# Block products that run on in two PSUM banks, running sums copied out by ScalarE, and low parts made in one piece

## The chip, the cores and the metric

The kernel runs on one core of a Trainium2 chip. The metric is device time in microseconds of one execution, the median of several runs. Lower is better.

## The reference, cut to what matters

Two branches over 2048 tokens of 576 features are mixed by a gate. One is a 2D Fourier filter. The other is a gated feed-forward layer with 4608 hidden features:

```python
x = A_x
g = _sigmoid((x * gate_w).sum(-1, keepdims=True))
a = irfft2(rfft2(x) * (A_w_r + 1j * A_w_i))
h = _gelu(B_x @ B_w_gate) * (B_x @ B_w_up)      # 2048 x 4608
b = h @ B_w_down                                # 2048 x 576
return g * a + (1 - g) * b
```

All inputs are fp32. The kernel splits an operand into a high part of 12 mantissa bits and a low part, the rest, and adds the products high x high, high x low and low x high.

## The kernel before, in words

Tokens stand in two halves of 1024, each as two groups (tb) of 512; hidden features in 36 tiles of 128. The first 900 us or so do the first token half plainly (all feature tiles), a few tiles of the second half, and the whole Fourier branch beside it on VectorE and ScalarE.

The rest of the second half is done in blocks, and only this stage is touched. A call of `products(i)`, for i = 5 to 17, takes two feature tiles and two token groups as a 2 x 2 block matrix product and does it with seven products in place of eight (a scheme of Winograd's kind): sums of the token side (a11, a12, a22, s1 to s4) were made once before, sums of the weight side are made block by block, and the four results c11, c12, c21, c22 are sums of products. Each product is done twice, for gate and for up (s = 0, 1), by `seven`: seven matmuls of 128x128 weights on 512 tokens into one PSUM bank. Six of them are high and low parts of two full feature tiles; the seventh takes the 64 features left over, high parts on partitions 0 to 63 and low parts on 64 to 127 (the tail). The weights stand in four slots of 1280 columns; `prep_b(i, m)` fills a slot two products ahead: `total` makes the weight sum on VectorE, `high` copies 768 columns to the rounded type on ScalarE, `low` makes the low parts on VectorE.

The banks are two of pool `pgu` and two of pool `pone`, taken in turn: product n uses the pair that product n - 2 used. VectorE adds each product to the running sums in SBUF (`add`, L1004). When a result is complete, `finish` queues gelu on the gate half (ScalarE), the multiplication by the up half (VectorE, L987), a rounded copy (ScalarE) and its low part (VectorE, L991). Behind a product come `downs`: a down is 12 matmuls of the hidden tiles of the block before on w_down into a pair of banks of pool `pdn` (L787), then a scaled copy out by ScalarE in `put` (L812) and an accumulating DMA from GpSimd's queue into the DRAM tile `yd` (L800). The last eight downs stand in `finale`: there the sums so far are loaded back from `yd` (`load_last`, SyncE's queue), VectorE adds to them in SBUF (L841), and SyncE's queue stores the result.

The order is written out by hand. Every engine executes its instructions in the order in which the program names them. `gap()`, called behind each half of a product and each down, counts up, and `seq(key, (n, step), ...)` names each step at the n-th gap from now (0 and 1 are both the next one); `due(key)` names what is left of a sequence at once.

Of the kernel before, what the change touches and what calls it, by code (L numbers as in the profile page):

```python
# [15 lines left out]
P = 128  # L16
# [15 lines left out]
FIRST = 5  # L32
# [125 lines left out]
def _build(nc, tc, a):  # L158
    with ExitStack() as ctx:
# [10 lines left out]
        def f(x):  # L170
            return x.bitcast(F32)
# [40 lines left out]
        def copy(o, i):  # L212
            act.activation(o, i, AF.Copy)  # L213
# [479 lines left out]
        def seq(key, *steps):  # L693

            q = todo[key] = [fn for _, fn in steps]
            for n, _ in steps:
                at(n, lambda: q and q.pop(0)())
# [264 lines left out]
        def seven(ps, i, m, x, s):  # L962

            due(("b", i, m))
            w, (xh, xl, xt) = slots[(7 * i + m) % 4], ops[x]
            hi, lo = w[:, 0:512], w[:, 768:1280]
            for t in range(2):
                c = slice(256 * t + P * s, 256 * t + P * (s + 1))
                pe.matmul(ps, hi[:, c], xh[:, t], start=t == 0, stop=False)  # L969
                pe.matmul(ps, lo[:, c], xh[:, t], start=False, stop=False)  # L970
                pe.matmul(ps, hi[:, c], xl[:, t], start=False, stop=False)  # L971
            pe.matmul(ps, w[:, 512 + P * s:512 + P * (s + 1)], xt, start=False, stop=True)  # L972
            tick(7 * 0.2265)
            gap()

        def products(i, spare, pend):

            j = NT + 2 * i
            u, c, u3 = gl, [xraw[:, q] for q in range(2)], [xraw[:, q] for q in range(2, 4)]
            made = {}  # L980

            def finish(name, x):
                h, (g, v) = spare.pop(0), x
                made[name] = h

                def mult():
                    vec.tensor_tensor(v, g, v, ALU.mult)  # L987
                    credit[0] -= 0.69

                def low():  # L990
                    vec.tensor_tensor(h[:, 1], v, f(h[:, 0]), ALU.subtract)  # L991
# [5 lines left out]
                if i == NT // 2 - 1 and name in ("c21", "c12"):  # L997
                    gelu()
                    seq((name, i), (1, mult), (1, lambda: copy(h[:, 0], v)), (2, low))
                else:  # L1000
                    seq((name, i), (1, gelu), (2, mult), (3, lambda: copy(h[:, 0], v)), (5, low))

            def add(o, x, v):
                vec.tensor_tensor(o, x, v, ALU.add)  # L1004
                credit[0] -= 0.69

            downs = (2, 2, 1, 1, 1, 1, 0) if i > FIRST else (1, 0, 1, 0, 1, 1, 0)
            for n, (name, nd) in enumerate(zip(("a11", "a12", "s2", "s3", "s1", "a22", "s4"), downs)):
                m = n + 2
                prep_b(i + m // 7, m % 7)  # L1010
                if n == 2:
                    for q in (0, 1, 3, 2):
                        load_b(i + 1, q)
                if n in (2, 3):
                    w = (j + n - 2) % 4
                    copy(dn[w][:, 0], wdr[n - 2])
                    lower(("dn", j + n - 2), dn[w], wdr[n - 2], 0.76)
                if n == 4:
                    due(("dn", j))
                    due(("dn", j + 1))  # L1020
                    load_d(i + 1)
                ps = [ps_one() if n % 2 else ps_gu() for _ in range(2)]
                for s in range(2):
                    seven(ps[s], i, n, name, s)
                    due({1: ("c12", i - 1), 3: ("c21", i - 1), 4: ("c11", i), 6: ("c22", i)}.get(n))
                    if n == 0:
                        copy(u[s], ps[s])
                    for o, x in (((), ((c, u),), ((u, u),), ((u3, u),), ((c, u3), (u, u)), ((u3, u3),), ((c, u),))[n]):
                        add(o[s], x[s], ps[s])
                k = {1: ("c11", c), 4: ("c22", c), 5: ("c21", u3), 6: ("c12", c)}.get(n)  # L1030
                if k:
                    finish(*k)
                for _ in range(nd):
                    if pend:
                        d, t = pend.pop(0)
                        down(d, t)
                        if t == 3 and len(d) > 4:
                            spare.extend(d[4])
                if i == NT // 2 - 1 and n == 5:
                    load_last(1)  # L1040
            for tb, names in ((1, ("c21", "c22")), (0, ("c11", "c12"))):
                hh = [made[q] for q in names]
                d = (1, i, tb, tuple((j + q, hh[q], (names[q], i)) for q in range(2)), hh)
                pend.extend((d, t) for t in range(4))

        def finale(pend):
            load_last(0)
            for d, t in pend[:4]:
                v = pair()
                for part in range(2):  # L1050
                    down_last(d, t, v, part)
                gap()
            d = pend[4][0]
            ps = [pair(), pair(), [ps_one()[:, 0:HD] for _ in range(2)], [ps_gu()[:, 0:HD] for _ in range(2)]]
            for part in range(2):
                for t in range(4):
                    down_last(d, t, ps[t], part)
# [197 lines left out]
```

## Time and profile before

| | |
|---|---|
| median of 3 runs | 1385.85 us (1384.22 to 1387.59) |
| span of the profiled execution | 1382.7 us; the page gives it no time of its own beside the span |
| TensorE busy | 1370.8 us, 99% |
| VectorE busy | 1119.5 us, 81% |
| ScalarE busy | 700.8 us, 51% |
| GpSimd busy | 265.4 us, 19% |

The span runs from the first to the last instruction; the rest of a run's time lies around it. PE is TensorE's matmuls, PEld its weight loads, DVE is VectorE, ACT ScalarE, POOL GpSimd, SP SyncE. Matmuls are pipelined: the duration of one is longer than the distance to the next.

### The profile page before, as it was taken

The numbers are of one execution on the slowest core, as the hardware profiler recorded it, in microseconds if no ns is written. First come the engines' busy times: TensorE is split into PE (matmuls) and PEld (weight loads), VectorE is DVE, ScalarE is ACT, GpSimd is POOL, SyncE is SP. The second block draws the span as 40 slices with busy tenths as digits, with TensorE's granted clock in tenths as the row PEclk, the third lists the DMA queues.
The fourth block names the chain that finished last, engine by engine and source line by source line (L and its number), as shares of the span: only waits on it lengthen the run. The fifth ranks groups of instructions, "written<-read, shape, count | busy, mean of one in ns | idle before, by whom it ended". The sixth has DMA issues, their size and how long they took to land.

```text
span 1382.7 us, 20005 instructions
## 1 busy us (share of the span) xinstructions
PE 1370.8 (99%) x7504; PEld 1211.0 (88%) x7504; DVE 1119.5 (81%) x1635; ACT 700.8 (51%) x1072; POOL 265.4 (19%) x326
## 2 busy tenths in 40 slices
PE   8999999999999999999999999999999999999998
PEld 7888888888888888888888888888888888888887
DVE  5999899989878877799988988557777777777776
ACT  5553443444566675543456345855555555555552
POOL 0022111122232221111113012321111121111110
PEclk9999999999999999999999999999999999999999
DMA  7366666657899997656678467966677777777776
GB/s 269 143 124 113 158 119 123 115 96 175 204 248 269 256 257 176 105 105 117 144 140 185 111 143 125 214 123 128 129 131 130 131 129 131 130 128 129 130 154 172
DMA packets 97330, 211.17 MB, mean 153 GB/s; under 512 B 11857, under 2 KB 22097, under 8 KB 96849
## 3 DMA queue, kind: packets, MB, share of 16 engines
q0 software_dynamic: 45248, 92.56, 44.4%
q1 hardware_dynamic: 51984, 117.34, 27.7%
q8 instruction: 59, 0.97, 0.3%
q14 instruction: 39, 0.31, 0.1%
HBM read 110.69 MB, written 92.01 MB: 147 GB/s over the span
## 4 chain that ended last, share of the span: by engine, by line
PE 85%; issue 6%; DVE 4%; ACT 1%; POOL 1%; DMA 1%; SPq 0%; DVEq 0%; POOLq 0%
PE pdn L787 29%; PE pgu L726 10%; PE pgu L728 10%; PE pgu L727 10%; PE pgu L969 3%; PE pgu L971 3%; PE pgu L970 3%; PE pone L969 3%; PE pone L971 3%; PE pone L970 3%; PE pgu L732 2%; PE pgu L733 2%; PE pgu L972 2%; PE pf L274 2%; PE pone L972 1%
## 5 line engine op out<-in xcount | busy, mean ns | idle before, releaser
L800 POOL DMA_DIRECT2D yd<-stg x264 | 229.1, 869 | 1043.4 <-ACT stg L812 922.0
L812 ACT ACTIVATE stg<-pdn,omg 128x576 f32<-128x576 f32 x272 | 201.7, 742 | 397.8 <-PE pdn L787 302.4
L787 PEld LDWEIGHTS pdn<-dn,hb 128*128 128x128 f32 x2808 | 388.6, 188 | 11.8 <-DVE raws L841 0.5
L787 PE MATMUL pdn<-dn,hb 128*128 128x288 f32 x2808 | 396.8, 295 | 0.2 <-DVE raws L841 0.2
L726 PE MATMUL pgu<-xhi,gu 128*128 128x512 f32 x728 | 285.5, 392 | 4.7 <-DVE gl L768 3.4
L728 PE MATMUL pgu<-xlo,gu 128*128 128x512 f32 x728 | 284.7, 391 | 0.0
L727 PE MATMUL pgu<-xhi,gu 128*128 128x512 f32 x728 | 284.3, 391 | 0.0
L726 PEld LDWEIGHTS pgu<-xhi,gu 128*128 128x128 f32 x728 | 137.1, 188 | 31.3 <-DVE gl L768 5.0
L728 PEld LDWEIGHTS pgu<-xlo,gu 128*128 128x128 f32 x728 | 137.1, 188 | 29.9
L727 PEld LDWEIGHTS pgu<-xhi,gu 128*128 128x128 f32 x728 | 136.9, 188 | 24.6
L213 ACT ACTIVATE hb<-gl 128x512 fp32r<-128x512 f32 x92 | 57.8, 628 | 111.0 <-DVE gl L768 110.6
L768 DVE TENSOR_TENSOR gl<-gl,pgu 128x512 f32<-128x512 f32 x92 | 62.9, 684 | 46.7 <-PE pgu L733 45.8
L764 ACT ACTIVATE gl<-pgu 128x512 f32<-128x512 f32 x91 | 54.3, 597 | 75.5 <-PE pgu L733 74.9
L213 ACT ACTIVATE gu<-raws 128x1280 fp32r<-128x1280 f32 (+3 forms) x86 | 88.6, 1031 | 5.9 <-DMA raws<-wgu 5.5
L787 PEld LDWEIGHTS pdn<-dn,gu 128*128 128x128 f32 x624 | 85.6, 188 | 1.9
L787 PE MATMUL pdn<-dn,gu 128*128 128x288 f32 x624 | 86.8, 295 | 0.0
L773 DVE TENSOR_TENSOR hb<-gl,hb 128x512 fp32r<-128x512 f32 x92 | 63.1, 686 | 16.5 <-ACT hb L213 16.5
L732 PE MATMUL pgu<-xtl,gu 128*128 128x512 f32 x182 | 70.9, 389 | 0.0
L733 PE MATMUL pgu<-xtl,gu 128*128 128x512 f32 x182 | 70.8, 389 | 0.0
L706 DVE TENSOR_TENSOR gu<-raws,gu 128x1280 fp32r<-128x1280 f32 x44 | 65.4, 1486 | 5.3 <-ACT gu L213 5.1
L987 DVE TENSOR_TENSOR xraw<-xraw 128x512 f32<-128x512 f32 x52 | 36.0, 693 | 28.8 <-ACT xraw L995 28.3
L1004 DVE TENSOR_TENSOR gl<-gl,pgu 128x512 f32<-128x512 f32 x52 | 35.6, 684 | 25.7 <-PE pgu L972 25.7
(213 smaller groups left out, 2214.6 us busy)
## 6 DMA issues: line engine op xcount, KB each, us to landing
yd<-stg POOLq DMA_DIRECT2D x264, 288.0 KB, 5.1
raws<-wgu SPq DMA_DIRECT2D x44, 640.0 KB, 4.9
raws<-wd SPq DMA_DIRECT2D x72, 288.0 KB, 2.9
colm<-col POOLq DMA_DIRECT2D x32, 256.0 KB, 6.2
raws<-ws SPq DMA_DIRECT2D x21, 384.0 KB, 6.0
quads<-ws SPq DMA_DIRECT2D x20, 384.0 KB, 4.2
tmp<-wf SPq DMA_DIRECT2D x16, 290.0 KB, 5.7
cns<-til SPq DMA_DIRECT2D x64, 72.5 KB, 5.4
```

Of the source, the lines that this page charges most:

```text
L213: act.activation(o, i, AF.Copy)
L726: pe.matmul(ps, w[:, 0, k, c], xhi[tb][:, k], start=k == 0, stop=False)
L727: pe.matmul(ps, w[:, 1, k, c], xhi[tb][:, k], start=False, stop=False)
L728: pe.matmul(ps, w[:, 0, k, c], xlo[tb][:, k], start=False, stop=False)
L732: pe.matmul(ps, w[:, 0, 4, c], xtl[tb], start=False, stop=False)
L733: pe.matmul(ps, w[:, 1, 4, c], xtl[tb], start=False, stop=True)
L787: pe.matmul(ps[half], h[:, l, c], d[:, q, half * HD:(half + 1) * HD], start=part == 0 and n == 0, stop=part == 1 and n == 2)
L800: pl.dma_start(yd[u], o, accum_op=ALU.add)
L812: put(u, lambda o: act.activation(o.rearrange("p (c k) -> p c k", c=2), v[:, :, 0:HD], AF.Copy, scale=omg[:, u:u + 1]), i == 0)
L969: pe.matmul(ps, hi[:, c], xh[:, t], start=t == 0, stop=False)
L970: pe.matmul(ps, lo[:, c], xh[:, t], start=False, stop=False)
L971: pe.matmul(ps, hi[:, c], xl[:, t], start=False, stop=False)
```

## The change

Four things change in the block stage. The order of the seven products and of the weight sums is another, and products run on: a11, s2, s3 and a22 add up in one pair of banks (b = 0), a12 in the other, which s1 and then s4 take over; from block to block the two pairs change places. Only the first product of a sum starts the bank anew. What was added in SBUF is now a sum in PSUM; where a running sum is wanted and the bank goes on, ScalarE copies it out (after products 0, 2 and 3), and VectorE adds only after products 1, 4 and 5. After the last product ScalarE takes the gelu straight from the bank, and VectorE multiplies by the other bank.

The slot's layout is low 0, high 0, tail, high 1, low 1 of 256 columns each, with the input tensor laid out to match. `high` copies 768 columns in the middle, `low` is one subtraction of 768 columns into pieces 0, 2 and 4, and a new step `tail`, one gap later, copies the high tail rows again on partitions 0 to 63 by ScalarE.

The downs stand behind other products, `finish` is called behind them, the weight loads for the next block one product later, and the two token groups of the finale change places, with the SBUF places that they are loaded to.

```diff
         def rest(i):
-            if i < 4:
-                return stg[i].rearrange("p c k -> p (c k)")
-            q = (2304, 2880, 1536, 0)[i - 4]
+            if i >= 4:
+                return stg[i - 4].rearrange("p c k -> p (c k)")
+            q = (2304, 2880, 0, 576)[i]
             return raws[:, q:q + D]
...
-            x = (r11, r21, tsum, r12, r11, r21, r22)[m]
+            x = (r11, r21, tsum, r11, r12, r22, r21)[m]
 
             def total():
-                for o, p, q in ((), (), ((r11, r12, r11), (tsum, r22, r11)), ((r12, r22, r12),), (),
-                                ((r21, r21, tsum),), ())[m]:
+                for o, p, q in ((), (), ((r11, r12, r11), (tsum, r22, r11)), (), ((r12, r22, r12),), (),
+                                ((r21, r21, tsum),))[m]:
                     vec.tensor_tensor(o, p, q, ALU.subtract)
                     credit[0] -= 0.95
 
             def high():
-                copy(w[:, 0:768], x)
+                copy(w[:, 256:1024], x)
 
             def low():
-                vec.tensor_tensor(w[:, 768:1280], x[:, 0:512], f(w[:, 0:512]), ALU.subtract)
-                vec.tensor_tensor(w[64:128, 512:768], x[64:128, 512:768], f(w[64:128, 512:768]), ALU.subtract)
-                credit[0] -= 1.15
-
-            seq(("b", i, m), (lead, total), (lead + 2, high), (lead + 4, low))
-
-        def seven(ps, i, m, x, s):
+                o = w.rearrange("p (c k) -> p c k", c=5)[:, 0:5:2]
+                vec.tensor_tensor(o, x.rearrange("p (c k) -> p c k", c=3),
+                                  f(w[:, 256:1024]).rearrange("p (c k) -> p c k", c=3), ALU.subtract)
+                credit[0] -= 0.95
+
+            def tail():
+                copy(w[0:64, 512:768], x[0:64, 256:512])
+
+            seq(("b", i, m), (lead, total), (lead + 2, high), (lead + 4, low), (lead + 5, tail))
+
+        def seven(ps, i, m, x, s, start, stop):
 
             due(("b", i, m))
             w, (xh, xl, xt) = slots[(7 * i + m) % 4], ops[x]
...
+            l0, h0, tl, h1, l1 = (w[:, 256 * q + P * s:256 * q + P * (s + 1)] for q in range(5))
+            for t, (hi, lo) in enumerate(((h0, l0), (h1, l1))):
+                pe.matmul(ps, hi, xh[:, t], start=start and t == 0, stop=False, skip_group_check=True)
+                pe.matmul(ps, lo, xh[:, t], start=False, stop=False, skip_group_check=True)
+                pe.matmul(ps, hi, xl[:, t], start=False, stop=False, skip_group_check=True)
+            pe.matmul(ps, tl, xt, start=False, stop=stop, skip_group_check=True)
             tick(7 * 0.2265)
             gap()
 
         def products(i, spare, pend):
...
+            c1, c2, c3 = gl, [xraw[:, q] for q in range(2)], [xraw[:, q] for q in range(2, 4)]
             made = {}
+            banks = [ps_gu, ps_one] if i % 2 else [ps_one, ps_gu]
...
-            downs = (2, 2, 1, 1, 1, 1, 0) if i > FIRST else (1, 0, 1, 0, 1, 1, 0)
-            for n, (name, nd) in enumerate(zip(("a11", "a12", "s2", "s3", "s1", "a22", "s4"), downs)):
+            downs = (0, 1, 1, 1, 2, 1, 2) if i > FIRST else (1, 1, 1, 1, 0, 0, 0)
+            ps = {}
+            for n, (name, nd) in enumerate(zip(("a11", "a12", "s2", "s1", "s3", "s4", "a22"), downs)):
                 m = n + 2
                 prep_b(i + m // 7, m % 7)
-                if n == 2:
+                if n == 3:
                     for q in (0, 1, 3, 2):
                         load_b(i + 1, q)
...
-                ps = [ps_one() if n % 2 else ps_gu() for _ in range(2)]
+                b = n % 2
+                if n in (0, 1, 3):
+                    ps[b] = [banks[b]() for _ in range(2)]
+                due({3: ("c22", i - 1), 6: ("c22", i)}.get(n))
                 for s in range(2):
-                    seven(ps[s], i, n, name, s)
-                    due({1: ("c12", i - 1), 3: ("c21", i - 1), 4: ("c11", i), 6: ("c22", i)}.get(n))
-                    if n == 0:
-                        copy(u[s], ps[s])
-                    for o, x in (((), ((c, u),), ((u, u),), ((u3, u),), ((c, u3), (u, u)), ((u3, u3),), ((c, u),))[n]):
-                        add(o[s], x[s], ps[s])
-                k = {1: ("c11", c), 4: ("c22", c), 5: ("c21", u3), 6: ("c12", c)}.get(n)
-                if k:
-                    finish(*k)
+                    v = ps[b][s]
+                    seven(v, i, n, name, s, n in (0, 1, 3), n in (1, 5, 6))
+                    if n in (0, 2, 3):
+                        copy({0: c1, 2: c2, 3: c3}[n][s], v)
+                    elif n in (1, 4, 5):
+                        o = {1: c1, 4: c3, 5: c2}[n][s]
+                        add(o, o, v)
+                    elif s == 0:
+                        act.activation(c3[0], v, AF.Gelu_apprx_tanh)
                 for _ in range(nd):
                     if pend:
                         d, t = pend.pop(0)
                         down(d, t)
                         if t == 3 and len(d) > 4:
                             spare.extend(d[4])
+                if n in (1, 4, 5):
+                    finish({1: "c11", 4: "c22", 5: "c12"}[n], {1: c1, 4: c3, 5: c2}[n])
+                elif n == 6:
+                    finish("c21", (c3[0], ps[b][1]), True)
                 if i == NT // 2 - 1 and n == 5:
-                    load_last(1)
-            for tb, names in ((1, ("c21", "c22")), (0, ("c11", "c12"))):
+                    load_last(0)
+            for tb, names in ((0, ("c11", "c12")), (1, ("c22", "c21"))):
...
         def finale(pend):
-            load_last(0)
+            load_last(1)
```

## Rows read from the trace of the kernel before

**Rows 1.** The page's busy time, share of the span and instructions by engine

```profile
PE 1370.8 (99%) x7504; PEld 1211.0 (88%) x7504; DVE 1119.5 (81%) x1635; ACT 700.8 (51%) x1072; POOL 265.4 (19%) x326
```

**Rows 2.** Busy time by engine, from 985 us on; then granted clock, DMA share

```profile
985.00:1382.70 397.70, 392.84 (x2197) 349.35 (x2195) 295.94 (x472) 192.78 (x292) 76.03 (x88) 1.00 0.71 134
```

**Rows 3.** The chain of waits from 915 us on: start, us, what

```profile
982.39 3.18 PE pdn L787 x24
...
1017.44 3.18 PE pdn L787 x24
```

**Rows 4.** Waits from 900 us on, TensorE's longest: total, times, longest us

```profile
PEld pdn L787 <- DVE raws L841: 0.5, 1, 0.5
```

**Rows 5.** Groups by line and shape from 985 us on: busy us, mean ns

```profile
L1004 DVE TENSOR_TENSOR gl<-gl,pgu 128x512 f32<-128x512 f32 x44 | 30.1, 684 | 22.8 <-PE pgu L972 22.8
...
L213 ACT ACTIVATE gl<-pgu 128x512 f32<-128x512 f32 x20 | 11.8, 589 | 8.3 <-PE pgu L972 8.3
...
L949 DVE TENSOR_TENSOR quads<-quads 128x768 f32<-128x768 f32 x10 | 9.6, 955 | 0.2
```

**Rows 6.** Timeline of matmuls and weight loads behind a down, 1030 us: start, us

```profile
1031.62 0.40 PE L969 MATMUL pone<-sx,gu 128*128 128x512 f32 x1
...
1033.00 0.39 PE L972 MATMUL pone<-sx,gu 128*128 128x512 f32 x1
...
1032.78 0.19 PEld L972 LDWEIGHTS pone<-sx,gu 128*128 128x128 f32 x1
```

**Rows 7.** Timeline of ScalarE at the same place

```profile
1031.87 0.74 ACT L812 ACTIVATE stg<-pdn,omg 128x576 f32<-128x576 f32 x1 [2.21 <-issue]
1032.51 0.67 ACT L213 ACTIVATE dn<-raws 128x576 fp32r<-128x576 f32 x1
```

**Rows 8.** ScalarE's groups by shape over the whole run: busy us, mean ns

```profile
L213 ACT ACTIVATE tmp<-til 64x580 f32<-64x580 f32 x16 | 11.0, 688 | 0.2
...
L213 ACT ACTIVATE gu<-raws 128x256 fp32r<-128x256 f32 x5 | 2.1, 417 | 4.0 <-DMA raws<-wgu 3.7
```

**Rows 9.** Timeline of all engines, 916.5 to 922.5 us (block 5, product 1)

```profile
918.62 0.96 DVE L949 TENSOR_TENSOR cns<-misc,raws 128x768 f32<-128x768 f32 x1
919.50 0.69 DVE L956 TENSOR_TENSOR gu<-raws,gu 128x512 fp32r<-128x512 f32 x1
...
920.13 0.40 PE L969 MATMUL pone<-xhi,gu 128*128 128x512 f32 x1
920.21 0.42 DVE L957 TENSOR_TENSOR gu<-raws,gu 64x256 fp32r<-64x256 f32 x1
920.24 0.19 PEld L970 LDWEIGHTS pone<-xhi,gu 128*128 128x128 f32 x1
920.36 0.39 PE L970 MATMUL pone<-xhi,gu 128*128 128x512 f32 x1
...
920.84 0.73 ACT L812 ACTIVATE stg<-pdn,omg 128x576 f32<-128x576 f32 x1
...
921.50 0.39 PE L972 MATMUL pone<-sx,gu 128*128 128x512 f32 x1
```

**Rows 10.** Busy time by engine in two short windows, and the wait before the second

```profile
170.00:180.00 10.00, 9.81 (x54) 8.31 (x52) 9.93 (x11) 2.66 (x4) 1.73 (x2) 1.00 1.01 210
...
744.00:748.00 4.00, 3.66 (x9) 2.91 (x10) 4.00 (x8) 2.25 (x4) 4.00 (x7) 0.59 1.07 165
...
PE pgu L726 <- DVE gl L768: 1.9, 1, 1.9
```

**Rows 11.** The finale: timeline of TensorE, VectorE, SyncE's queue; loads: KB, us to landing

```profile
1359.73 8.04 SPq L832 DMA_DIRECT2D stg<-yd  x3
1359.86 1.75 PE L787 MATMUL pdn<-dn,hb 128*128 128x288 f32 x12
...
1375.71 1.79 DVE L841 SCALAR_TENSOR_TENSOR stg<-pdn,omg,stg 128x288 f32<-128x288 f32 x4 [3.55 <-PE pdn L787]
...
stg<-yd SPq DMA_DIRECT2D x4, 288.0 KB, 3.3
```

More of the change, by code (lines that the diff above doesn't have):

```diff
@@ L952, in high @@
             def high():
-                copy(w[:, 0:768], x)
+                copy(w[:, 256:1024], x)
             def low():
-                vec.tensor_tensor(w[:, 768:1280], x[:, 0:512], f(w[:, 0:512]), ALU.subtract)
-                vec.tensor_tensor(w[64:128, 512:768], x[64:128, 512:768], f(w[64:128, 512:768]), ALU.subtract)
-                credit[0] -= 1.15
-            seq(("b", i, m), (lead, total), (lead + 2, high), (lead + 4, low))
-        def seven(ps, i, m, x, s):
+                o = w.rearrange("p (c k) -> p c k", c=5)[:, 0:5:2]
[6 more added lines that the diff above has]
+        def seven(ps, i, m, x, s, start, stop):
             due(("b", i, m))
             w, (xh, xl, xt) = slots[(7 * i + m) % 4], ops[x]
[L966 to L972, printed above, removed]
+            l0, h0, tl, h1, l1 = (w[:, 256 * q + P * s:256 * q + P * (s + 1)] for q in range(5))
[4 more added lines that the diff above has]
+            pe.matmul(ps, tl, xt, start=False, stop=stop, skip_group_check=True)
             tick(7 * 0.2265)
@@ L978, in products, with finish @@
             j = NT + 2 * i
-            u, c, u3 = gl, [xraw[:, q] for q in range(2)], [xraw[:, q] for q in range(2, 4)]
+            c1, c2, c3 = gl, [xraw[:, q] for q in range(2)], [xraw[:, q] for q in range(2, 4)]
             made = {}
-            def finish(name, x):
+            banks = [ps_gu, ps_one] if i % 2 else [ps_one, ps_gu]
+            def finish(name, x, done=False):
                 h, (g, v) = spare.pop(0), x
@@ L986, in mult @@
                 def mult():
-                    vec.tensor_tensor(v, g, v, ALU.mult)
+                    vec.tensor_tensor(g, g, v, ALU.mult)
                     credit[0] -= 0.69
                 def low():
-                    vec.tensor_tensor(h[:, 1], v, f(h[:, 0]), ALU.subtract)
+                    vec.tensor_tensor(h[:, 1], g, f(h[:, 0]), ALU.subtract)
                     credit[0] -= 0.69
@@ L995, in gelu @@
                     act.activation(g, g, AF.Gelu_apprx_tanh)
-                if i == NT // 2 - 1 and name in ("c21", "c12"):
-                    gelu()
-                    seq((name, i), (1, mult), (1, lambda: copy(h[:, 0], v)), (2, low))
+                if done:
+                    seq((name, i), (0, mult), (1, lambda: copy(h[:, 0], g)), (2, low))
                 else:
-                    seq((name, i), (1, gelu), (2, mult), (3, lambda: copy(h[:, 0], v)), (5, low))
+                    seq((name, i), (1, gelu), (2, mult), (3, lambda: copy(h[:, 0], g)), (5, low))
             def add(o, x, v):
@@ L1038, in products @@
                             spare.extend(d[4])
+                if n in (1, 4, 5):
+                    finish({1: "c11", 4: "c22", 5: "c12"}[n], {1: c1, 4: c3, 5: c2}[n])
+                elif n == 6:
+                    finish("c21", (c3[0], ps[b][1]), True)
                 if i == NT // 2 - 1 and n == 5:
-                    load_last(1)
-            for tb, names in ((1, ("c21", "c22")), (0, ("c11", "c12"))):
+                    load_last(0)
+            for tb, names in ((0, ("c11", "c12")), (1, ("c22", "c21"))):
                 hh = [made[q] for q in names]
-                d = (1, i, tb, tuple((j + q, hh[q], (names[q], i)) for q in range(2)), hh)
+                js = (j, j + 1) if tb == 0 else (j + 1, j)
+                d = (1, i, tb, tuple((js[q], hh[q], (names[q], i)) for q in range(2)), hh)
                 pend.extend((d, t) for t in range(4))
         def finale(pend):
-            load_last(0)
+            load_last(1)
             for d, t in pend[:4]:
@@ L1225 @@
     half = np.stack([np.concatenate([np.arange(256) + 256 * h] + [np.arange(512, 544) + 32 * h] * 4) for h in range(2)])
+    side = np.concatenate([half[:, 0:128], half[:, 256:384], half[:, 128:256]], 1)
     xs = xT[half][:, :, tok[1]].reshape(2, 3, P, 2, TB).transpose(3, 0, 2, 1, 4)
-    ws = np.stack([w[half].reshape(2, 3, P, NT, P) for w in (wg, wu)]).transpose(4, 1, 3, 2, 0, 5)
+    ws = np.stack([w[side].reshape(2, 3, P, NT, P) for w in (wg, wu)]).transpose(4, 1, 3, 2, 0, 5)
     ws = ws.reshape(NT, 2, P, 768)
```

## The prediction

> **What bounds the kernel now.** I read the page first: of a span of 1382.7 us TensorE is busy 99%, VectorE 81%, ScalarE 51% [rows 1]. A busy share of matmuls can hide a slow stream, so the window over the last stage comes next [rows 2]. From 985 us on, the granted clock is 1.00 (the 2.4 GHz level) and TensorE is idle for 397.70 - 392.84 = 4.9 us, most of it after its last matmul. The change touches only this stage: block products, 13 calls of products (i = 5 to 17), seven products each. The chain of waits shows whether anything but TensorE sets the pace there. It is TensorE all the way, and it repeats: the double group of down matmuls at 982.39 comes back at 1017.44 [rows 3]. One block takes 35.05 us. The work in it is 98 product matmuls and 96 down matmuls. From the rows, 12 down matmuls take 3.18/2 = 1.59 us [rows 3], and seven product matmuls about 7 x 0.227 = 1.59 us (the seventh of a half starts 1.38 after the first, [rows 6]). So 14 halves x 1.59 + 8 downs x 1.59 = 35.0 us: the whole period. There is no wait in a block that a lighter VectorE could give back. The waits of TensorE after 900 us confirm it: the longest is 0.5 us, once, in the finale [rows 4].
>
> **What the change removes.** Eight of 14 adds a block go: 8 x 0.684 = 5.5 us of VectorE [rows 5]. The low part becomes one piece of 768 columns in place of 512 plus a second, 64-partition piece; nearest price of the new piece is the 128x768 subtraction, 0.955 us [rows 5]. All of it lay beside matmuls, so on the path this is worth nothing; even everything TensorE waits for after 900 us is under 1 us [rows 4]. The number of matmuls, LDWEIGHTS and transfers is the same, and so is the number of switches between products and downs in a block (six, one behind each of six products).
>
> **What it adds.** ScalarE gets four more PSUM copies a block, 4 x 0.589 = 2.4 us [rows 5], and seven tail copies (64 partitions, 256 columns). The trace has no 64x256 copy; a 128x256 one takes 0.417 us, and a 64x580 one 0.688 against 0.67 for a 128x576 one, so fewer partitions do not shorten a copy [rows 7, 8]. I take 0.417: 2.9 us a block. ScalarE is busy 192.78 of 397.70 us in the stage [rows 2], that is 17.0 us a block; with 5.3 more it has 22 of 35. It does not become the bound. Its order can: a copy of ScalarE now stands between VectorE's low part and the matmul that reads the tail, and it stands in one queue with put (L812), which waits for the down matmuls.
>
> **Where a bank is read late.** A product that runs on in the banks of the product two before it must wait for the copy of the running sum. Between the two lies always one whole product, 3.2 us, and the copy takes 0.6; the same distance held for the adds before. The third product of a block, for instance, starts 8 us after the first and needs only the first's copies. The last product's gelu is read from its bank at once and its mult follows after one gap; those banks are needed again by the second product of the next block, which 2 downs and a product (6.4 us) separate. So I cost the shared banks at nothing, and their cover is one product.
>
> **The tail copy, product by product.** prep_b(i, m) is called two products ahead; high comes at the second gap after the call, low at the fourth, tail at the fifth. A gap follows each half (seven) and each down. With the new downs (0,1,1,1,2,1,2) the fifth gap falls within the product before the one that uses it, or earlier in the one before that, for all but m = 2. It is called in product 0, which has no down: gaps 1 and 2 are there, 3 and 4 in product 1's halves, and gap 5 is the one behind product 1's down. There the tail copy is queued behind that down's put. Let P be the start of product 2's first matmul. In the same position before, P = 1031.62, put starts at 1031.87 = P + 0.25 and the next ScalarE instruction at 1032.51 = P + 0.89 [rows 6, 7]. So the tail ends at P + 0.89 + 0.417 = P + 1.31. The seventh matmul's LDWEIGHTS reads it, and starts at P + 1.16, its matmul at P + 1.38 [rows 6].
>
> How much a late LDWEIGHTS costs is seen once: at 920.24 that of L970 waited for the low part L956 (919.50 + 0.69 = 920.19, so 0.05 from end to start), 0.11 after the first matmul at 920.13, and its matmul still started in step at 920.36, only 0.12 behind it [rows 9]. So about 0.1 us of lateness is free. Here: LDWEIGHTS at P + 1.31 + 0.05 = 1.36, matmul at 1.48 in place of 1.38: a stall of 0.10 us. A full queue of TensorE gives nothing back afterwards. Blocks 6 to 17 have it: 12 x 0.10 = 1.2 us. Bounds: nothing if the copy is 0.1 shorter, 0.2 each (2.4 us) if a late LDWEIGHTS is paid in full.
>
> **The first blocks.** Block 5 has other downs (1,1,1,1,0,0,0), and three places get tight.
> - Product 1 of block 5. Its low part is forced out when the product begins; L956 started at 919.50 and ended just in time [rows 9]. In one piece it ends at 919.50 + 0.955 = 920.46, LDWEIGHTS 920.51, matmul 920.63 for 920.36: 0.27. Its tail is queued behind the put at 920.84, so it starts at 920.84 + 0.64 = 921.48 and ends at 921.90; the seventh matmul comes at 922.07 for 921.50 + 0.27: 0.30 more [rows 9].
> - Product 6 of block 5. No down lies between products 4, 5 and 6, so the low part follows the first add of product 5. That add starts 1.4 us before product 6, takes 0.6 to the next start, then 0.955: the end is 0.18 after the product's first matmul, 0.12 late by the rule above.
> - Product 1 of block 6. No down follows product 6 of block 5 or product 0 of block 6. VectorE has, after product 6's end, the mult (0.6), two subtractions (0.96 and 0.88, the second by the starts at 918.62 and 919.50 [rows 9]) and then this low part (0.955). It starts some 0.4 after product 0 does, when the product's last sum is drained and the adds before are done, so that ends at 0.4 + 3.4 = 3.8; with the 0.05 and less the free 0.1 it is wanted at 3.2: about 0.55.
> Sum 1.24 us; bounds 0.3 and 2.2.
>
> **The finale.** Two downs now follow the last product, so the last sums into yd are issued later and the loads of the second half wait for them. Before, the load's queue stood until 1359.73 + 8.04 = 1367.77, which is 6.3 us after the end of the last down before it (1359.86 + 1.59 = 1361.45). With the finale beginning right behind the last down, that is 6.3 into it, and 3.3 us to land gives 9.6; the first add that needs one came at 1375.71, 11.1 us after the finale's start (1361.45 and one product, 1364.64) [rows 11]. Hidden, with 1.5 us of cover; the first-half loads are issued three products' time earlier than they are needed. Stores behind the loads wait 3 us longer and need not. Cost 0, bound 1 us.
>
> **Sum.** 1.2 + 1.24 = 2.4 us on the span of 1382.7: 1385.1. The profiled execution has no time of its own on the page beside the span; the median of the runs shown, 1385.85, is 3.15 above the span, and I keep that: 1388.3 us, 0.18% above the median. Under 0.2% (2.8 us) a measurement of this kernel cannot tell it from no change.
>
> **Rivals.**
> - No stall: the tails come in time, TensorE stays full. For it: the margins are tenths of a us. Then 1385.85, at most 0.9 less [rows 4].
> - Slower: product 2 is held as a whole. If its first LDWEIGHTS (0.13 before P) waited for the tail, the first matmul came at P + 1.36 + 0.12 in place of P: 1.48 x 12 = 17.8, with the first blocks 1404.9. Against it: at 920.24 LDWEIGHTS went ahead while L957 was still to write another part of the same slot, so waits go by part [rows 9]. It decides from the point where the wait sits on a matmul ahead of the sixth.
> - Slower: the clock. From 744 to 748 the granted clock averaged 0.59, between the two levels, after TensorE had stood for 1.9 us; 4 x (1 - 0.59) = 1.6 us of matmul time lost [rows 10]. If each of the 15 blocks or places with a stall did that: 24 + 2.4 us, 1412. Against it: 170 to 180 has 0.19 us of idle time at clock 1.00 [rows 10]. The Trainium skill (TensorE: Matmul & The Clock Gate, "A second HAM failure mode: psum-queue depth-cycling") says that short idle times between groups that cycle through PSUM banks make the clock swing; by it this would be the outcome, and the row at 1.00 speaks against it for stalls this short.
> - Faster by over 0.2%: TensorE's own pace would have to rise with fewer adds on PSUM. No row shows a pace that depends on VectorE.
>
> **How the numbers follow.** Small stalls as summed 0.62 (own range 1386.5 to 1390.5; two in five of it above 0.2%), none 0.22, whole product held 0.05, clock 0.03, faster 0.08. Slower: 0.25 + 0.05 + 0.03 = 0.33; same 0.37 + 0.22 = 0.59; faster 0.08. The range takes in the first two cases with the bounds (1385.85 + 4.6 and the finale's 1; below, 0.9 and the runs' own spread of 1.6): 1384.0 to 1391.5.
>
> **What would show it.** A period of 35.15 in blocks 6 to 17, with one short wait of TensorE on the tail copy at product 2's seventh matmul, and three waits between 920 and 948 us; VectorE near 20 us busy a block, ScalarE near 22. The prediction is wrong if the period stays 35.05, if a product's first matmul waits, or if the finale's adds wait for a transfer.

## The result, and the profile after

The changed kernel takes 1387.66 us (median of 16 runs, 1385.35 to 1389.50), the kernel before 1384.61 us (16 runs, 1383.09 to 1387.59). The ratio of the runs is 1.0019, with a 95% interval of 1.0012 to 1.0027: some 2.6 us (1.7 to 3.7) slower. The forecast was 1388.3 us, 2.45 above the median of 1385.85 that it started from. The profiled execution of the changed kernel took 1385.35 us with a span of 1383.5.

A difference this small drowns in a span of which the first 900 us differ from run to run: in the profiles below the changed stage begins anywhere from 913.5 to 917.1 us. So the changed stage is measured by itself, in each profile: from the first product matmul of block 5 to the finale's start. In the kernel before the timeline and the chain of waits give the two ends:

```profile
915.37 0.39 PE L969 MATMUL pgu<-xhi,gu 128*128 128x512 f32 x1
...
1364.80 6.40 PE pdn L787 x48
```

After the change two downs run into the finale's, so that of the 72 down matmuls in one piece the last 48 are the finale's:

```profile
914.13 0.39 PE L972 MATMUL pgu<-xhi,gu 128*128 128x512 f32 x1
...
1362.40 9.60 PE pdn L787 x72
```

The finale starts at 1362.40 + 9.60 x 24/72 = 1365.60. The stage took 449.43 us before and 451.47 after: **2.04 us more**. From the finale's start to the span's end both take 17.9 us. The spans differ by only 0.8 because the stage of the changed kernel happened to begin 1.24 us earlier, which is the first part's doing.

The window over the last stage answers to [rows 2]:

```profile
985.00:1383.50 398.50, 393.63 (x2207) 349.35 (x2205) 227.34 (x309) 235.45 (x410) 76.25 (x88) 1.00 0.69 134
```

VectorE's busy time fell from 295.94 to 227.34 us, ScalarE's rose from 192.78 to 235.45. The granted clock is 1.00 again, and TensorE is idle for 398.50 - 393.63 = 4.9 us, as before, so no long wait lies behind 985 us. (A matmul lasts 0.39 us and the next starts 0.227 behind it, so a stall of up to some 0.16 does not show as idle time; the period of the blocks, below, shows it.) The waits of TensorE's weight loads after 910 us, where the kernel before has only the row of 0.5 us in [rows 4] (columns: total, times, longest):

```profile
PEld pgu L975 <- ACT gu L213: 1.6, 7, 0.6
PEld pone L975 <- ACT gu L213: 1.4, 7, 0.4
PEld pgu L973 <- DVE gu L957: 0.9, 2, 0.6
PEld pdn L787 <- DVE raws L841: 0.5, 1, 0.5
PEld pone L973 <- DVE gu L957: 0.3, 1, 0.3
```

Only weight loads that read a tail (L975, from ScalarE) or a low part (L973, from VectorE) wait. None waits for a bank, and the finale's one wait is unchanged. Fourteen waits are on tails: eleven of 0.17 in the later blocks and three more ahead of 985 us. All waits on low parts stand there too. The timeline of weight loads from 918 to 954 us shows them (idle time in brackets):

```profile
919.26 0.19 PEld L973 LDWEIGHTS pone<-xhi,gu 128*128 128x128 f32 x1 [0.31 <-DVE gu L957]
920.68 0.19 PEld L975 LDWEIGHTS pone<-sx,gu 128*128 128x128 f32 x1 [0.41 <-ACT gu L213]
940.38 0.19 PEld L973 LDWEIGHTS pgu<-xhi,gu 128*128 128x128 f32 x1 [0.26 <-DVE gu L957]
941.95 0.19 PEld L975 LDWEIGHTS pgu<-s,gu 128*128 128x128 f32 x1 [0.58 <-ACT gu L213]
947.66 0.19 PEld L973 LDWEIGHTS pgu<-xhi,gu 128*128 128x128 f32 x1 [0.60 <-DVE gu L957]
953.62 0.19 PEld L975 LDWEIGHTS pone<-sx,gu 128*128 128x128 f32 x1 [0.17 <-ACT gu L213]
```

The first two are product 1 of block 5, the next two product 6, then product 1 of block 6; 953.62 is the first of the twelve small ones at product 2 of blocks 6 to 17. What each costs is read from the matmuls around it, which otherwise start 0.227 apart. The fourth, for instance, in the timeline of TensorE, ScalarE and VectorE:

```profile
940.24 0.69 DVE L991 TENSOR_TENSOR xraw<-xraw 128x512 f32<-128x512 f32 x1
...
940.96 0.63 ACT L213 ACTIVATE gu<-xraw 128x512 fp32r<-128x512 f32 x1 [2.23 <-DVE xraw L991]
...
941.41 0.40 PE L974 MATMUL pgu<-xlo,gu 128*128 128x512 f32 x1
941.50 0.40 ACT L213 ACTIVATE gu<-raws 64x256 fp32r<-64x256 f32 x1
...
942.29 0.40 PE L972 MATMUL pgu<-xhi,gu 128*128 128x512 f32 x1
```

ScalarE waited 2.23 us, with the tail copy next but one, because the rounded copy of c22 ahead of it waits for VectorE's multiplication L991. The two matmuls around the seventh start 942.29 - 941.41 = 0.88 apart in place of 0.453, two steps of 0.227: a stall of 0.43.

| place | weight load idle | stall |
|---|---|---|
| product 1 of block 5, low part | 0.31 | 0.26 |
| the same, tail | 0.41 | 0.25 |
| product 6 of block 5, low part | 0.26 | 0.11 |
| the same, tail | 0.58 | 0.43 |
| product 1 of block 6, low part | 0.60 | 0.46 |
| product 2 of blocks 6 to 17, tail | 0.17 | 0.03 each, 12 x 0.03 = 0.36 |

They sum to 1.87 of the 2.04 us. Part of the rest stands right behind the stalls, where a few matmuls start 0.23 to 0.24 apart: the seven from 942.29 to 943.92 take 1.63 in place of 1.59. The 0.03 is from the period of the blocks, by the chain of waits:

```profile
986.00 1.58 PE pdn L787 x12
...
1021.08 1.58 PE pdn L787 x12
...
1056.17 1.58 PE pdn L787 x12
```

The period is (1056.17 - 986.00)/2 = 35.085, where it was 35.05 [rows 3].

### The profile page after: what moved, and what is told of

Its sections match the earlier page's. It is cut to its first block, busy times and chain, and to the rows that moved or that the text cites. A ratio compares the mean times of both kernels' runs of the same rounds, so it can differ in the third digit from the quotient of the medians.

```text
span 1383.5 us, 19831 instructions
## 1 busy us (share of the span) xinstructions
PE 1370.6 (99%) x7504; PEld 1208.1 (87%) x7504; DVE 1038.4 (75%) x1440; ACT 752.7 (54%) x1215; POOL 266.1 (19%) x326
## 4 chain that ended last, share of the span: by engine, by line
PE 84%; issue 7%; DVE 4%; DMA 2%; POOL 1%; ACT 1%; SPq 1%; DVEq 0%; POOLq 0%; ACTq 0%
PE pdn L787 28%; PE pgu L726 10%; PE pgu L728 9%; PE pgu L727 9%; PE pgu L973 3%; PE pgu L972 3%; PE pgu L974 3%; PE pone L972 3%; PE pone L973 3%; PE pone L974 3%; PE pgu L732 2%; PE pgu L733 2%; PE pgu L975 2%; PE pf L274 2%; PE pone L975 1%
## 5 line engine op out<-in xcount | busy, mean ns | idle before, releaser
L787 PE MATMUL pdn<-dn,hb 128*128 128x288 f32 x2892 | 413.0, 295 | 0.0
L787 PEld LDWEIGHTS pdn<-dn,hb 128*128 128x128 f32 x2892 | 402.0, 188 | 11.8 <-DVE hb L773 0.2
L213 ACT ACTIVATE hb<-gl 128x512 fp32r<-128x512 f32 x102 | 64.0, 628 | 114.4 <-DVE gl L768 114.1
L213 ACT ACTIVATE gu<-raws 64x256 fp32r<-64x256 f32 (+3 forms) x121 | 101.6, 850 | 7.2 <-DMA raws<-wgu 5.7
L768 DVE TENSOR_TENSOR gl<-gl,pgu 128x512 f32<-128x512 f32 x92 | 62.9, 683 | 44.9 <-PE pgu L733 44.4
L787 PE MATMUL pdn<-dn,gu 128*128 128x288 f32 x540 | 83.6, 295 | 0.2 <-DVE raws L841 0.2
L787 PEld LDWEIGHTS pdn<-dn,gu 128*128 128x128 f32 x540 | 76.7, 188 | 1.9 <-DVE raws L841 0.5
L706 DVE TENSOR_TENSOR dn<-raws,dn 128x576 fp32r<-128x576 f32 x72 | 54.1, 752 | 1.3 <-ACT dn L213 1.3
L92 DVE TENSOR_TENSOR rows<-rows 128x1280 f32<-128x1280 f32 x36 | 53.5, 1487 | 0.5
```

Source lines behind the costliest of these rows:

```text
L706: vec.tensor_tensor(g[:, 1], r, f(g[:, 0]), ALU.subtract)
L787: pe.matmul(ps[half], h[:, l, c], d[:, q, half * HD:(half + 1) * HD], start=part == 0 and n == 0, stop=part == 1 and n == 2)
```

## The experiments

The theory after this: the whole loss is weight loads that wait for late copies in ScalarE's and VectorE's queues, three quarters of it (1.51 us) in blocks 5 and 6; the shared banks cost nothing, and the lighter VectorE gives nothing. Rivals: the shared banks or the new order of downs cost something by themselves; or a stall that is taken away comes back at the next wait. The stage is measured as above (449.43 before, 451.47 after), in one profile of each kernel. It repeats well: a second profile of the changed kernel gave 451.49, and two kernels below whose stage is that of another and only the first part differs gave 449.43 for 449.43 and 449.55 for 449.57. So differences of a tenth can be read. Ratios are to the kernel before on the same chip.

| kernel | stage, us | against before | ratio (95%) |
|---|---|---|---|
| the change | 451.47 | +2.04 | 1.0019 (1.0012 to 1.0027) |
| old_layout | 450.35 | +0.92 | 1.0008 (0.9999 to 1.0017) |
| layout_alone | 450.04 | +0.61 | 1.0005 (0.9996 to 1.0015) |
| tail_with_low | 451.04 | +1.61 | 1.0009 (1.0000 to 1.0018) |
| first_blocks_moved | 450.26 | +0.83 | 1.0003 (0.9994 to 1.0013) |
| all_moved | 449.57 | +0.14 | 1.0006 (0.9997 to 1.0014) |
| tail_twice | 457.99 | +8.56 | 1.0059 (1.0045 to 1.0072) |
| tail_ahead_of_c22 | 450.99 | +1.56 | one run |
| product2_tail_early | 451.14 | +1.71 | one run |

layout_alone and before_two_gaps start from the kernel before, all others from the changed one. The edit of old_layout is cut to its main lines.

**old_layout.** The shared banks and the new order of products and downs, with the slot's old layout, two-piece low part and no tail copy.

```diff
-                copy(w[:, 256:1024], x)
+                copy(w[:, 0:768], x)
...
-            seq(("b", i, m), (lead, total), (lead + 2, high), (lead + 4, low), (lead + 5, tail))
+            seq(("b", i, m), (lead, total), (lead + 2, high), (lead + 4, low))
```

> Stage length is counted from the first product matmul of block 5 to the finale's start: 449.4 us before, 451.45 us after, 2.05 us more. Theory (late copies of low parts and tails hold single LDWEIGHTS): with the old slot layout and no tail copy the waits on tails go (0.25 + 0.43 + 12 x 0.03 = 1.04 us) and the two-piece low part is 0.27 us earlier at three places, which leaves about 0.2 us at product 1 of block 6. Stage 449.6 us, 0.2 us over before, ratio 1.000. Rival (the shared banks and ScalarE's copies of running sums cost it): stage stays at 451.4 us, ratio 1.0015.

Measured: 450.35, between the two, 0.75 above the theory's 449.6. Every wait on a tail is gone, and so are the waits at products 1 and 6 of block 5, but at product 1 of block 6 a longer one stands, in the timelines of weight loads and matmuls:

```profile
946.52 0.19 PEld L970 LDWEIGHTS pgu<-xhi,gu 128*128 128x128 f32 x1 [1.06 <-DVE gu L956]
```

```profile
945.50 0.39 PE L969 MATMUL pgu<-xhi,gu 128*128 128x512 f32 x1
946.52 0.50 PE L970 MATMUL pgu<-xhi,gu 128*128 128x512 f32 x1 [0.63 <-DVE gu L956]
946.86 0.40 PE L971 MATMUL pgu<-xlo,gu 128*128 128x512 f32 x1
```

That is a stall of 946.86 - 945.50 - 0.453 = 0.91, all of the +0.92. It is not the layout's: with no down behind product 6 of block 5 and product 0 of block 6, VectorE has one instruction behind the other from 939.54 to this low part at 945.78, which has 512 columns and lasts 0.69. TensorE comes there earlier than in the changed kernel (31.80 us after the stage's start in place of 32.96), and waits longer.

**layout_alone.** The kernel before with the new layout, the low part in one piece and the tail copy; products, banks and downs as they were. The edit is the reverse of the one above, in the kernel before.

> The kernel before with the new slot layout, one-piece low part and tail copy; banks, adds, order of products and downs as before. Theory of late copies: product 1 of block 5 loses 0.26 us on its low part and 0.25 us on its tail, the other places have downs enough: stage 449.9 us, 0.5 us over before, ratio 1.000. If the new layout costs by itself whatever the order, 451 us. If the shared banks cost it all, 449.4 us with no wait at product 1 of block 5.

Measured: 450.04, near the theory's 449.9. There is the wait on a low part (0.31) and the one on a tail (0.43) at product 1 of block 5, and two waits of 0.17 on tails later in block 5 that were not foreseen. Taken by itself the layout costs 0.61, the new order 0.92. The 2.04 of both is not their sum: only together do they have a tail behind a down's put in every block (0.36) and one behind c22's copy (0.43), while the stall at product 1 of block 6 is half as long once TensorE comes there later.

**tail_with_low.** The tail copy at the low part's gap.

```diff
-            seq(("b", i, m), (lead, total), (lead + 2, high), (lead + 4, low), (lead + 5, tail))
+            seq(("b", i, m), (lead, total), (lead + 2, high), (lead + 4, low), (lead + 4, tail))
```

> The changed kernel with the tail copy named at the same gap as the low part, ahead of the down's put in ScalarE's queue. Theory of late copies: the twelve waits of 0.03 us at product 2 and the 0.43 us at product 6 of block 5 go, the rest (0.26 + 0.25 + 0.11 + 0.46) stays: stage 450.65 us, 1.25 us over before. Shared banks: 451.45 us, unchanged. ScalarE may then wait for VectorE's low part for up to 1 us at a time; if that comes through, the stage gets longer.

Measured: 451.04, a gain of 0.43 where 0.82 was expected. The small waits of all later blocks and the tail wait at product 6 are gone, but product 1 of block 6 now waits 0.90 in place of 0.60, and product 0 of block 6 has a wait of 0.26 on its low part that was not there. By the matmuls around them these cost 0.30 and 0.10 more, which is the gain that is handed back.

**all_moved and first_blocks_moved.** In the first, the tail at the low part's gap, block 5's downs between the products that were short of them, and the preparation for product 1 of block 5 named four gaps earlier. The second has the same but for the first line of the edit.

```diff
-            seq(("b", i, m), (lead, total), (lead + 2, high), (lead + 4, low), (lead + 5, tail))
+            seq(("b", i, m), (lead, total), (lead + 2, high), (lead + 4, low), (lead + 4, tail))
...
-            downs = (0, 1, 1, 1, 2, 1, 2) if i > FIRST else (1, 1, 1, 1, 0, 0, 0)
+            downs = (0, 1, 1, 1, 2, 1, 2) if i > FIRST else (1, 0, 0, 0, 1, 1, 1)
...
-                prep_b(i + 1, 1)
+                prep_b(i + 1, 1, -4)
```

> The changed kernel with three moves: tail copy at the gap of the low part, block 5's downs (1,0,0,0,1,1,1) in place of (1,1,1,1,0,0,0), and the second weight product of block 5 prepared four gaps earlier. Theory of late copies: no product waits any more; stage 449.4 us as before, ratio 1.000 (0.9993 to 1.0007). Shared banks: 451.4 us, ratio 1.0015. Clock theory (the runs differ by dips of the granted clock, the waits bring more of them): runs of this one lie like those of before, at 0.998 to 1.000.

> The changed kernel with only the first blocks mended: block 5's downs (1,0,0,0,1,1,1) and the second weight product of block 5 prepared four gaps earlier; the tail copy stays one gap behind the low part. Theory of late copies: the four places in blocks 5 and 6 (1.25 us) go, the twelve waits of 0.03 us at product 2 stay: stage 449.6 + 0.36 = 449.95 us against 451.47 of the changed kernel and 449.57 with everything moved. Rival (what is left is spread over all blocks, by the banks or by ScalarE's load): 451 us.

Measured: 449.57 for the first, 450.26 for the second. In all_moved one wait of 0.25 on a low part is left, at product 1 of block 6, and no tail is waited for:

```profile
PEld pgu L973 <- DVE gu L957: 0.3, 1, 0.3
```

With shared banks, ScalarE's copies and the new layout all in place, the stage is as long as before to within 0.14 us, and 0.11 of that is the stall at the wait that is left. So banks and copies are free where they are in time. It is not shorter either, though VectorE has a fourth less to do. first_blocks_moved came out 0.31 above its expectation: the new downs make a wait of 0.62 on a tail at 927.73 us (product 3 of block 5), which was not foreseen and costs 0.46. With no down behind products 1 and 2 this tail too is named only when its product begins, behind other copies on ScalarE; in all_moved it is named a gap earlier. The median of first_blocks_moved says nothing against the stage's lengths, and can't: all ratios from 1.0003 to 1.0009 have intervals that overlap.

**tail_twice.** Each tail copy made twice.

```diff
                 copy(w[0:64, 512:768], x[0:64, 256:512])
+                copy(w[0:64, 512:768], x[0:64, 256:512])
```

> The changed kernel with each tail copy made twice, one behind the other; the second ends about 0.31 us later (0.40 less the 0.09 by which two copies overlap). Theory of late copies: product 2 of blocks 6 to 17 waits 0.34 us in place of 0.03, and product 1 and 6 of block 5 wait 0.31 longer: stage 451.47 + 12 x 0.31 + 0.6 = 455.8 us; the other five products of a block show nothing, though ScalarE does 2.1 us more in every block. Rival (ScalarE's load as such costs): the loss is spread over all products. Rival (tails are hidden): 451.5 us.

Measured: 457.99, +6.52 on the change and 2.2 above what was expected: each block is 0.46 longer than the changed kernel's in place of 0.31, by the chain's period of 35.55, since the second copy ends 0.45 behind the place where the single one ended. The chain of waits goes where the prediction put it, through put and the tail copies to the seventh matmul of product 2:

```profile
1025.88 1.60 PE pdn L787 x12
1027.47 0.02 issue
1027.50 0.74 ACT stg L812
1028.24 0.31 ACT gu L213
...
1028.57 0.42 ACT gu L213
...
1029.04 0.50 PE pone L976
```

The weight load of 1029.04 stood idle for 0.62, and the stall is 0.46. Against the changed kernel (0.17 and 0.03) the lateness grew by 0.45 and the stall by 0.43: past the free part, all of it is paid, and none is given back before the next block.

**tail_ahead_of_c22.** One swap in ScalarE's order: the tail copy ahead of c22's rounded copy, at product 6 of block 5. The line stands in every product, but by the count of gaps this is the only place where a tail copy is still to be named when c22's copy is called up.

```diff
+                due(("b", i, n))
                 due({3: ("c22", i - 1), 6: ("c22", i)}.get(n))
```

> The changed kernel with one swap in ScalarE's order: at product 6 of block 5 the tail copy goes ahead of the rounded copy of c22. The theory is that the 0.58 us wait at that product's seventh matmul is paid because the tail copy stands behind a copy that waits for VectorE's mult. Then the wait disappears, VectorE's work behind it moves up by the same time, and the stage from product 0 of block 5 to the finale takes 451.47 - 0.43 = 451.04 us. The rival, that the time saved comes back as a longer wait at product 1 of block 6 (as it did with the old layout and with the tail moved to the low part's gap), gives 451.4 to 451.5 and a wait there over 0.9 us in place of 0.60.

Measured: 450.99, a gain of 0.48. The tail copy starts right behind its low part, by the timeline of ScalarE, and the wait of 0.58 is gone:

```profile
939.76 0.42 ACT L213 ACTIVATE gu<-raws 64x256 fp32r<-64x256 f32 x1 [1.99 <-DVE gu L957]
940.36 0.63 ACT L213 ACTIVATE gu<-xraw 128x512 fp32r<-128x512 f32 x1 [0.18 <-DVE xraw L991]
```

Product 1 of block 6 waits 0.60 as before. Nothing was handed back here, because VectorE's queue moved up by as much: its low part for that product starts at 945.59, 1.06 earlier, of which 0.60 is this run's earlier start of the stage.

**product2_tail_early.** The tail of product 2 one gap earlier, ahead of put, in blocks 6 to 17 alone.

```diff
-            seq(("b", i, m), (lead, total), (lead + 2, high), (lead + 4, low), (lead + 5, tail))
+            seq(("b", i, m), (lead, total), (lead + 2, high), (lead + 4, low), (lead + (4 if m == 2 and i > FIRST else 5), tail))
```

> The changed kernel with product 2's tail copy one gap earlier, ahead of put, in blocks 6 to 17 alone; the first blocks are left as they are. The theory puts 0.03 us on each of these twelve stalls: 12 x 0.03 = 0.36, so the stage takes 451.1 us with a period of 35.055. The rival is the prediction's own term, 0.10 each: 450.3. No wait on a tail copy is left after 953 us.

Measured: 451.14, a gain of 0.33, so 0.03 for each of the twelve. The period is back at 35.05, by the chain of waits:

```profile
989.01 1.58 PE pdn L787 x12
...
1024.07 1.58 PE pdn L787 x12
...
1059.12 1.58 PE pdn L787 x12
```

**all_moved_two_gaps and before_two_gaps.** The largest wait of TensorE after the start is not in the changed stage but at 744 us [rows 10], in the first part. Two empty gaps between the two halves of the inverse rotation there, added to all_moved and, in another kernel, to the kernel before:

```diff
-            for h in range(2):
-                yield from inverse_rows(h)
+            yield from inverse_rows(0)
+            for _ in range(2):
+                yield None
+            yield from inverse_rows(1)
```

> The kernel with all three moves, and two empty gaps between the two inverse row transforms, so that a multiplication of the main stage at 745 us is not named behind VectorE's writes that wait for ScalarE. Stage as before, 449.6 us. TensorE's wait of 2.0 us near 745 us goes, and with it the fall of the granted clock that follows it in some executions (1.6 us): ratio 0.9975 to 0.9985 of before, and runs that lie closer together. If the mult is held by something else, the wait stays at 2 us and the ratio at 1.000.

> The kernel before, with two empty gaps between the two halves of the inverse rotation of the first part, and nothing of the change. The theory is that the gain of the version with all copies moved and the two gaps comes from the gaps alone, through the stand of 1.9 us at 744 us and the clock behind it: ratio 0.9975 to 0.9985, a median near 1382, no wait of TensorE over 1.1 us at 744 us. The rival, that the gain needs the shared banks or the moved copies, gives 0.9995 to 1.0005.

Measured: with all_moved 1381.93 us (11 runs), ratio 0.9982 (0.9973 to 0.9991), faster than both kernels. With the kernel before 1382.30 us (11 runs), ratio 0.9989 (0.9979 to 0.9998). The windows from 740 to 748 us of the two, TensorE busy throughout:

```profile
740.00:748.00 8.00, 8.00 (x41) 6.79 (x40) 6.70 (x13) 7.75 (x12) 5.12 (x10) 1.00 0.74 117
```

```profile
740.00:748.00 8.00, 8.00 (x37) 6.61 (x36) 6.42 (x12) 8.00 (x12) 3.62 (x7) 1.00 0.79 153
```

The gain needs the two gaps and nothing of the change. It shows in the medians, not in the profile of the second kernel, whose changed stage begins at 915.36, no earlier than at 915.37 in the kernel before: there the clock was low near the start of the run (last section). The second came out a little under its expectation; whether the moved copies add anything to the gaps can't be told from two intervals that overlap.

**after_again.** The changed kernel as it is, a second profile.

> The changed kernel once more, for how well the stage length repeats. Stage 451.4 to 451.6 us with the same five waits over 0.1 us; the span may lie anywhere from 1383 to 1388 us, by what the granted clock does in the first 900 us.

Measured: 451.49, with the same waits to 0.1 us in total.

## Why the prediction was right, step by step

**Bound.** Right. TensorE sets the pace of the stage in all profiles, and 5.5 us less of adds a block bought nothing: all_moved, without the stalls, is not below the kernel before.

**Shared banks at nothing.** Right: no wait for a bank in any profile of the stage, and all_moved has them at +0.14, of which 0.11 is a stall on a low part.

**The tail of product 2, 12 x 0.10.** Right in place and mechanism, mis-sized: 12 x 0.03. It is the chain put, tail, seventh weight load that was named, in the timeline of all engines:

```profile
1022.50 0.40 PE L972 MATMUL pone<-sx,gu 128*128 128x512 f32 x1
...
1022.70 0.74 ACT L812 ACTIVATE stg<-pdn,omg 128x576 f32<-128x576 f32 x1 [3.42 <-PE pdn L787]
...
1023.34 0.40 ACT L213 ACTIVATE gu<-cns 64x256 fp32r<-64x256 f32 x1
...
1023.80 0.19 PEld L975 LDWEIGHTS pone<-sx,gu 128*128 128x128 f32 x1 [0.17 <-ACT gu L213]
1023.89 0.41 PE L975 MATMUL pone<-sx,gu 128*128 128x512 f32 x1
...
1024.14 0.40 PE L972 MATMUL pone<-sx,gu 128*128 128x512 f32 x1
```

With P = 1022.50, put starts at P + 0.20 (0.25 was read off a neighbouring place) and the weight load at P + 1.30 (1.36 in the sum), its matmul at P + 1.39 in place of 1.38, and the next one 0.25 behind it in place of 0.227. Some 0.14 us of a weight load's idle time is free, where the prediction had read 0.1 off one row. Three readings of a few hundredths each decided a term of 0.10; the low bound, nothing, was nearer than the value taken.

**The first blocks, 1.24.** Four terms, each measured: the low part of product 1 of block 5 0.27 forecast, 0.26 measured; its tail 0.30 and 0.25; the low part of product 6 0.12 and 0.11; product 1 of block 6 0.55 and 0.46. **A fifth was missed**: the tail of product 6 of block 5, 0.43. The step that failed is the entry "Product 6 of block 5" in the list of tight places: it costs the low part and puts the tail at nothing without a word. The count that cleared the tails ("the fifth gap falls within the product before the one that uses it, or earlier") was made with the downs of the later blocks. In block 5 no down lies behind products 4 and 5, so the fifth gap would come within product 6 itself, and the tail copy is named only when product 6 begins. `due` of c22 stands ahead of it there, so that c22's rounded copy, which waits for VectorE, goes first on ScalarE. tail_ahead_of_c22 shows this by the swap alone.

**The sum.** 2.4 forecast, 2.04 measured in the stage, where 0.84 too much for product 2 and 0.43 too little at product 6 partly cancel, and 0.16 too much in the other four terms meets 0.17 that lies at no place of the table. That it lies so near is in part luck. So is the time, 1388.3 for 1387.66: the three runs that it started from had a median 1.24 above that of all 16. The range's lower end, 1384.0, is not the sum of what is named for it (1385.85 - 0.9 - 1.6 = 1383.35). And the limit of 0.2%, under which a change could not be told from none, was too wide: 16 runs each told 0.19%, with 0.12% as the lower bound.

**The finale and its loads at nothing.** Right. SyncE's queue stands until 1360.61 + 11.74 = 1372.35, 6.75 us into the finale where 6.3 was forecast:

```profile
1360.61 11.74 SPq L832 DMA_DIRECT2D stg<-yd  x4
```

The first add that needs a load of the second half starts at 1376.51, 10.91 us into the finale as before, and TensorE's one wait there is the same 0.5.

**Product 2 held as a whole.** Fell: the matmuls ahead of the one that reads the tail go on while it is still to come. At 1022.50, above, the first of them starts before the tail copy does.

**The clock.** Fell. Windows around the stalls, TensorE's busy time first, the granted clock third from the end:

```profile
918.00:922.00 4.00, 4.00 (x20) 2.91 (x20) 2.86 (x4) 3.30 (x6) 0.86 (x1) 1.00 0.00 0
938.00:944.00 6.00, 5.86 (x26) 4.32 (x25) 4.92 (x7) 3.70 (x7) 0.00 (x0) 1.00 0.92 258
944.00:949.00 5.00, 4.82 (x22) 3.67 (x21) 4.59 (x6) 4.11 (x8) 0.00 (x0) 1.00 0.54 198
```

The clock is 1.00 in each, behind stalls of up to 0.46. In tail_twice, with that stall in each of twelve blocks, the window over nearly the whole stage has it at 1.00 too:

```profile
917.00:1370.00 453.00, 449.41 (x2444) 392.02 (x2443) 263.43 (x348) 312.87 (x574) 86.36 (x102) 1.00 0.65 130
```

The rule of the Trainium skill that the prediction weighed (TensorE: Matmul & The Clock Gate, "A second HAM failure mode: psum-queue depth-cycling") speaks of short idle times between groups of matmuls. The windows do not bear it out for stalls this short, which lie within groups of seven.

**What should show it.** The period was 35.085, not 35.15; VectorE was busy 20.0 us a block (227.34 x 35.085/398.50), as forecast, ScalarE 20.7 in place of 22; five waits between 918 and 948 us, not three.

What stays open: the runs differ by 2.6 us (1.7 to 3.7), the stage by 2.04, of which 1.87 has a place. That fits, but whether the last half microsecond is real is not settled, since the runs of one kernel spread over 4 us.

## What to carry to other kernels

Where an engine's order is written by hand, a copy is as late as the slowest thing named ahead of it on its engine: follow that queue for every consumer, above all at the first and the last round of a loop, where the pattern of fillers differs; here five places in two blocks cost four times as much as twelve rounds of the steady state. A stall taken away may come back at the next full queue, as in tail_with_low, or not, as in tail_ahead_of_c22; so look at the next wait behind it too. And read a saving by the stage's own length: work taken off an engine that nothing waits for was worth nothing here, while two empty gaps at the one long wait of the first part gave 0.11% (0.02 to 0.21) by themselves.

## What was not expected of the hardware

A late weight load has a free part, and it is steady and somewhat larger than the 0.1 us forecast. The stall was the weight load's idle time less 0.14 to 0.16 us in seven places of three kernels: 0.17 gave 0.03, 0.26 gave 0.11, 0.41 gave 0.25, 0.58 gave 0.43, 0.60 gave 0.46, 0.62 gave 0.46, 1.06 gave 0.91. Only the first after a down was dearer, 0.31 for 0.26.

The clock answers one and the same wait differently from run to run. TensorE stands 1.9 to 2.0 us just ahead of 744.5 us in the kernel before and in the changed one. In the profile of the first the granted clock then averaged 0.59 from 744 to 748 us [rows 10]. Of the two profiles of the changed kernel, the same program, the first kept 1.00 and the second (after_again) fell to 0.57:

```profile
744.00:748.00 4.00, 3.31 (x14) 2.74 (x15) 4.00 (x9) 2.49 (x5) 4.00 (x8) 1.00 1.01 146
...
744.00:748.00 4.00, 4.00 (x11) 3.13 (x12) 4.00 (x7) 2.09 (x4) 4.00 (x7) 0.57 1.10 158
```

With the two gaps the wait is gone and the clock 1.00 there in both profiles. So a wait in the first part that the change doesn't touch is one source of the spread of the runs, which is larger than the effect to be measured.

The start of the run is a second source. From 10 to 20 us the clock was 1.00 in both profiles of the changed kernel, but 0.83 in those of all_moved, tail_twice and product2_tail_early, whose changed stages begin latest of all (916.77 to 917.11 us), and 0.73 in that of before_two_gaps:

```profile
10.00:20.00 10.00, 7.22 (x22) 5.13 (x22) 6.97 (x11) 5.15 (x9) 0.00 (x0) 0.73 1.06 374
```
